# Local attention moved from GpSimd to TensorE and ScalarE, and q and k projected eight heads at a time

## The chip, the core and the metric

The kernel runs on one core of a Trainium2 chip. The core has five engines with a queue of instructions each, which run side by side and wait for one another by semaphores: TensorE (PE in the profile; PEld is its loading of weights), VectorE (DVE), ScalarE (ACT), GpSimd (POOL) and SyncE (SP), which here only issues DMAs. TensorE reads its operands from SBUF and writes into PSUM; a matmul can use a part of the array only, so that several small ones in different rows or columns run side by side. The metric is the device time of one execution in microseconds, as the median of several executions.

## The reference

```
x [1, 2048, 512];  32 heads of 16;  W, dil = 8, 2
g = sigmoid((x * gate_w).sum(-1))
a = A_ref(x, A_wqkv, A_wo)      # full attention, softmax over all 2048 keys
b = B_ref(x, B_wqkv, B_wo)      # local attention:
    idx = pos[:, None] - (arange(W) * dil)[None, :]     # 8 keys: s, s-2, ..., s-14
    logits = einsum("bhsd,bhswd->bhsw", q, k[idx]) * scale, -1e9 where idx < 0
    o = einsum("bhsw,bhswd->bhsd", softmax(logits), v[idx]);  b = o @ wo
out = g * a + (1 - g) * b
```

All arrays are bfloat16. A token of the local part sees only tokens of its own parity.

## The kernel before

**The global part** is cut into 32 periods: four chunks of 512 queries (`QW`) times eight groups of four heads (`NG`). A period has 16 tiles of 128 keys, so 64 units of one head's scores, 128 keys x 512 queries; the kernel has 2048 units. The scores are matmuls of 32 rows, one head in each quarter of the array. 16 of a head's 32 rows hold the head's dimensions; one further row carries a bound on the score in q and ones in k, so that no maximum over the keys is needed. A unit's exponential is taken by one of two engines. ScalarE does it exactly, three or two units at once out of two PSUM rings (`ring`, result `pT`). VectorE approximates it for four units at once, a quad (`make_quad`, lines 1310 to 1355): four conversions of scores into the bit pattern of a bfloat16 (`conv`, `dt<-m_ps`), then two added offsets (`term`, `dt<-dt`), the three versions being summed by the matmuls with V under weights (`WTS`, `vd_all`). At most `TD` = 4 of a period's 16 key tiles can go this way. The probabilities go into a matmul with V and a column of ones, 17 columns of the array for each head, into one PSUM bank (`acc`); `post` (line 912) turns the result, divides it by the sum (on GpSimd) and turns it back.

**Projections.** `k_proj` (line 520) and `q_proj` (line 619) do four heads at a time, each head's 16 columns in its own column quarter of the array. q also needs its magnitude (`absq`) and a second matmul with `selk` for the bound. `v_proj` (line 573) uses the full array.

**The local part** goes by 16 tiles of 128 tokens (`b_tile`, line 700). k, v and q are projected token-wise; k and v are stored to HBM (`kv_scr`) and loaded again eight times shifted (`ksh`, `vsh`, 1 MB each). GpSimd then multiplies, adds up trees, subtracts the maximum, normalises and weighs v, some 36 instructions a tile; VectorE gives the maximum, sum and reciprocal, ScalarE one small exp. The result (`obb`) is transposed by TensorE (`fin2`, `fin3`) and goes into `final` (line 962), which projects both parts with the output weights, mixes them by the gate and stores them.

**Order.** The class `Sched` (lines 118 to 328) is a planner that runs while the kernel is built. Every operation has an engine, an assumed duration, dependences, slots of buffers it takes and gives back, and a due time; the planner keeps a clock for each engine, always emits the operation that can start first, and among those that are near it the one due first. The order that comes out is the order of each engine's queue. `pe_source`, `act_source` and `d_source` offer the units of the attention: a fill of a ring for ScalarE (`fillA`) is due when ScalarE runs dry, and `start_quad` (line 1278) begins a quad when VectorE has less than 3 us of work waiting, fewer than three quads are under way and no TensorE operation is overdue. `warm` adds matmuls with zeros (`zero_pass`) where TensorE's recent streaming falls under a set share. `hooks(p)` (line 1388) runs when period p begins and sets up the projections and local tiles of later periods with due times in units of `TPER`, the planner's length of a period. Two PSUM banks (`m`) serve all other matmuls: projections, conversions and finals.

All instructions are recorded through one helper, so the profile shows line 382 (L382) for nearly all of them; groups are told apart by the names of their tiles.

Of the kernel before, what the change touches and what calls it, by code (L numbers as in the profile page):

```python
# [18 lines left out]
H = 32  # L19
# [5 lines left out]
NEG = -1.0e9  # L25
INF = 10 ** 12
# [7 lines left out]
TD = 4  # L34


def _mean_log_ratio():
    n = 4096
    acc = 0.0
    for k in range(n):  # L40
        y = 128.0 * k / n
        s = 0.0
        for o, w in zip(OFFS, WTS):
# [15 lines left out]
          ("ACT", "DVE"): 1000.0, ("DVE", "POOL"): 800.0, ("SP", "POOL"): 1500.0, ("POOL", "ACT"): 1000.0}  # L59
# [58 lines left out]
class Sched:  # L118
# [115 lines left out]
    def best(self, e):  # L234
# [14 lines left out]
        near = [c for c in cands if max(free, c[1]) <= soonest + 60.0]  # L249
# [82 lines left out]
def kernel(  # L332
# [13 lines left out]
    out2d = out.flatten_outer_dims()  # L346
    S, D = x2d.shape
# [56 lines left out]
    KEPT = 11  # L404
    for name_, n_ in (("m", 2), ("rA", 1), ("rB", 1), ("acc", 1), ("pTA", 3), ("pTB", 3), ("qt", 3), 
                      ("dt", 8), ("accT", 2), ("ott", 2), ("ksv", 2), ("prod", 1), ("lg", 2),
                      ("kvs", 1), ("qb", 1), ("osb", 3), ("keep", KEPT + 16), ("fb", 1)):
        S_.slots[name_] = Slots(n_)
# [15 lines left out]
    e32 = const.tile([128, 32], BF16, name="e32")  # L424
    V.memset(e32[:], 0.0)
    V.memset(e32[0:1, DH:DH + 1], 1.0)
    selq = const.tile([128, 128], BF16, name="selq")
    V.memset(selq[:], 0.0)
    for j in range(4):
        V.memset(selq[32 * j:32 * j + DH, 32 * j + DH:32 * j + DH + 1], 1.0)  # L430
    ident = const.tile([128, 128], BF16, name="ident")
    make_identity(nc, ident[:])

    wq = const.tile([128, DC, D], BF16, name="wq")
    wkv = const.tile([128, DC, 2 * D], BF16, name="wkv", tag="wkv")
    gw = const.tile([128, DC], BF16, name="gw")
    bw = const.tile([128, DC, 3 * D], BF16, name="bw")
    bwo = const.tile([128, DC, D], BF16, name="bwo")
# [4 lines left out]
    kmax_all = const.tile([128, NG, NC], FP32, name="kmax_all")  # L443
    kmax = const.tile([128, NG], FP32, name="kmax")
    selk_all = const.tile([128, NG, 128], BF16, name="selk_all")
    gate = const.tile([128, NT], FP32, name="gate")
    omg = const.tile([128, NT], FP32, name="omg")
    kv_scr = tc.dram_tile([16 + S, 2 * D], BF16, name="kv_scr")

    G.memset(vp_all[:, :, :, DH:DH + 1], 1.0)  # L450
    S_.t["POOL"] = 9000.0
# [6 lines left out]
    def x_load(half):  # L458

        def s():  # L460
            lo, hi = half * S // 2, (half + 1) * S // 2
            for c in range(DC):
                SP.dma_start(out=xT[:, c, lo:hi], in_=x2d[lo:hi, c * 128:(c + 1) * 128], transpose=True)
        return s
# [11 lines left out]
    for name, o, lo in (("wk0", wkv[:, :, 0:G1], D), ("wq0", wq[:, :, 0:G1], 0), ("wv0", wkv[:, :, D:D + G1], 2 * D)):  # L476
        with nc.allow_non_contiguous_dma(reason="columns of one head group"):
            A.dma_start(out=o, in_=a_w3[:, :, lo:lo + G1])
        ld[name] = S_.add(Op("SP", lambda: None, dur=1.0, due=-10.0, lat=4500.0, name=f"ld_{name}"))
    load("x0", x_load(0), 8100.0)  # L480
    load("x1", x_load(1), 11500.0)
    load("wv", dma(wkv[:, :, D + G1:2 * D], a_w3[:, :, 2 * D + G1:3 * D]), 9000.0)
    load("wk", dma(wkv[:, :, G1:D], a_w3[:, :, D + G1:2 * D]), 9000.0)
    load("wq", dma(wq[:, :, G1:D], a_w3[:, :, G1:D]), 9000.0)
# [5 lines left out]
    load("bw", dma(bw[:], B_wqkv.rearrange("(c p) n -> p c n", p=128)), 12000.0)  # L490

    def pad_load():
        for k in range(2 * D // 128):
            SP.dma_start(out=kv_scr[0:16, 128 * k:128 * k + 128], in_=zw[0:16, :])
    ld["pad"] = S_.add(Op("SP", pad_load, dur=4500.0, due=2000.0, lat=3000.0, name="ld_pad"))
    ld["bwo"] = S_.add(Op("SP", dma(bwo[:], B_wo.rearrange("(c p) n -> p c n", p=128)), dur=1500.0, due=2100.0, lat=6000.0, name="ld_bwo"))
    wo = []

    def wo_jobs(deps):

        def get():
            wo.append(const.tile([128, NG // 2, D], BF16, name="woarr", tag="wkv"))
# [15 lines left out]
    kt_ops = {}  # L518

    def k_proj(i, sc, due, first=False):  # L520
        hold = Hold("m")
        st = {}

        def part(c0, c1):
            def s():
                if c0 == 0:
                    st["pk"] = misc_ps(hold, [128, QW])
                    mm_init(st["pk"], e32, QW)
                pk = st["pk"]
                for c in range(c0, c1):  # L530
                    for j in range(4):
                        h = 4 * i + j
                        mm(pk[32 * j:32 * j + DH, :], wkv[:, c, h * DH:(h + 1) * DH],
                           xT[:, c, sc * QW:(sc + 1) * QW], False, c == DC - 1, tile_position=(0, 32 * j))
            return s

        def evac():
            o = kt_all[:, i, sc * QW:(sc + 1) * QW]
            if first:
                A.copy(out=o, in_=st["pk"][:])  # L540
            else:
                V.tensor_copy(out=o, in_=st["pk"][:])

        def red():
            src = st["pk"][:] if first else kt_all[:, i, sc * QW:(sc + 1) * QW]
            V.tensor_reduce(out=kmax_all[:, i, sc:sc + 1], in_=src, axis=AX.X, op=ALU.max, apply_absolute_value=True)
        slow = 2 if first and sc == 0 else 1
        p1 = Op("PE", part(0, 2), mms=COL4 * (3 * slow), deps=xt_ops[sc] + [ld["wk0" if i == 0 else "wk"]], due=due, acq=[hold], not_before=0.0 if first else due - 5000.0,
                name="k1")
# [928 lines left out]
```

## Time and profile before

| | us |
|---|---|
| median of three runs | 804.42 (801.79 to 805.17) |
| the profiled execution, its own time | 798.02 |
| its span, first to last instruction | 796.0 |
| TensorE's mean granted clock | 0.992 |
| GpSimd: sums and products for local attention (`prod`, three largest groups) | 268.9 + 161.7 + 152.2 |
| TensorE: local projections (768 matmuls), busy | 55.6 |
| TensorE: q projections (496 matmuls), busy | 36.0 |
| DMA traffic | 47.46 MB, mean 60 GB/s |

Busy time is the time in which at least one instruction of the group was running. Instructions of one engine overlap a little at their ends, and a matmul's 0.38 us are mostly its way through the array, while the next ones already stream; so a busy TensorE isn't a full one, and the distance from start to start says more.

### The profile page before, as it was taken

Reading aid. Unit: us, or ns where it says so; the run is one execution under the profiler, and the core shown is the slowest. Engines: PE = TensorE matmul, PEld = TensorE weight load, DVE = VectorE, ACT = ScalarE, POOL = GpSimd, SP = SyncE. Lnnn points to the kernel's source line nnn. Section 1 sums busy time; section 2 is a strip of 40 time slices with the busy share of each in tenths; the row PEclk is TensorE's granted clock in tenths of the full one; section 3 lists DMA queues with packets and bytes.
Section 4 is the critical chain, followed back from the end, with each engine's and each line's share of the span. In section 5 each row is a group of like instructions: output and inputs, shape, how many; then the busy total and the mean of one; then the engine's idle time right before and its main releaser. Section 6 shows DMA issues by size and latency. Waiting matters only on the chain.

```text
span 796.0 us, 20219 instructions
## 1 busy us (share of the span) xinstructions
PE 738.2 (93%) x8481; PEld 237.4 (30%) x8481; DVE 676.4 (85%) x1013; ACT 756.2 (95%) x680; POOL 695.4 (87%) x599
## 2 busy tenths in 40 slices
PE   7999999999999989999989899999999989999996
PEld 2332222333232223333322222333222222222222
DVE  3369899888989998989997888978998898888985
ACT  2899999899999999999999999999999999999993
POOL 1019799999999999999899999999998999999896
PEclk9799999999999999999999999999999999999999
DMA  9220321032011212111111121101122210122100
GB/s 206 88 68 12 109 67 55 18 104 68 22 47 54 68 54 68 55 50 42 45 68 54 54 67 54 65 18 55 56 67 81 68 54 30 53 68 67 61 15 34
DMA packets 52074, 47.46 MB, mean 60 GB/s; under 512 B 12048, under 2 KB 49424, under 8 KB 51984
## 3 DMA queue, kind: packets, MB, share of 16 engines
q1 hardware_dynamic: 50400, 45.98, 18.6%
q8 instruction: 66, 1.08, 0.6%
q10 hardware_dynamic: 1584, 0.20, 0.2%
q14 instruction: 24, 0.20, 0.1%
HBM read 37.75 MB, written 6.32 MB: 55 GB/s over the span
## 4 chain that ended last, share of the span: by engine, by line
ACT 29%; PE 28%; DVE 16%; POOL 16%; issue 9%; SPq 1%; DMA 0%; POOLq 0%; DVEq 0%; ACTq 0%
ACT pT L382 29%; POOL prod L382 13%; PE m_ps L382 13%; DVE dt L382 11%; PE acc L382 8%; PE ring L382 7%; SPq L382 1%; POOL lg L382 1%; DVE accT L382 1%; POOL obb L382 1%; POOL ott L382 0%; DVE kt_all L382 0%; DMA xT<-in_A_x_dram 0%; DVE kvs L382 0%; DVE vd_all L382 0%
## 5 line engine op out<-in xcount | busy, mean ns | idle before, releaser
L382 ACT ACTIVATE pT<-ring 128x1536 bf16<-128x1536 f32 (+1 forms) x658 | 750.1, 1316 | 13.2 <-PE ring L382 11.8
L382 PE MATMUL ring<-qt,kt_all 32*128 32x512 bf16 x1644 | 278.0, 383 | 31.0 <-ACT pT L382 25.3
L382 POOL TENSOR_TENSOR prod<-prod 128x512 f32<-128x512 f32 x224 | 295.2, 1324 | 10.8
L382 DVE TENSOR_SCALAR dt<-m_ps 128x512 uint16<-128x512 f32 x404 | 265.3, 676 | 26.8 <-PE m_ps L382 17.5
L382 DVE TENSOR_SCALAR dt<-dt 128x2048 uint16<-128x2048 uint16 x202 | 224.5, 1116 | 1.6 <-PE acc L382 1.0
L382 PEld LDWEIGHTS <-kt_all 32*128 32x128 bf16 (+1 forms) x2304 | 98.1, 91 | 293.1 <-issue 280.8
L382 POOL TENSOR_TENSOR prod<-ksh,qb 128x512 f32<-128x512 bf16 x128 | 161.7, 1292 | 5.6 <-DMA ksh<-kv_scr 3.3
L382 PE MATMUL acc<-pT,vp_all 128*17 128x512 bf16 x1644 | 158.1, 384 | 0.0
L382 POOL TENSOR_TENSOR prod<-vsh,lg 128x512 f32<-128x512 bf16 x128 | 152.2, 1208 | 3.5
L382 PE MATMUL m_ps<-qt,kt_all 32*128 32x512 bf16 x404 | 135.6, 381 | 5.8 <-DVE dt L382 4.5
L382 POOL TENSOR_TENSOR ott<-accT,rden 128x256 bf16<-128x256 f32 x31 | 25.0, 807 | 60.9 <-DVE rden L382 60.8
L382 PEld LDWEIGHTS <-vp_all 128*17 128x17 bf16 x2048 | 46.0, 88 | 107.4 <-issue 99.2
L382 PE MATMUL acc<-dt,vd_all 128*17 128x512 bf16 x808 | 61.1, 379 | 0.0
L382 PE MATMUL m_ps<-bw,xT 128*32 128x512 bf16 x768 | 55.6, 382 | 3.2 <-DVE dt L382 2.0
L382 PE MATMUL acc<-ones_t,zw 128*32 128x512 bf16 (+1 forms) x235 | 51.2, 391 | 1.3 <-DVE accT L382 1.2
L382 PEld LDWEIGHTS <-xT 128*32 128x32 bf16 (+1 forms) x1152 | 32.5, 97 | 32.9 <-issue 26.5
L382 PE MATMUL acc<-dt,vp_all 128*17 128x512 bf16 x404 | 39.6, 383 | 0.0
L382 PE MATMUL m_ps<-xT,wkv 128*16 128x512 bf16 x512 | 38.3, 388 | 1.2 <-DMA xT<-in_A_x_dram 1.2
L382 PE MATMUL m_ps<-xT,wq 128*16 128x512 bf16 x496 | 36.0, 380 | 0.0
L382 DVE TENSOR_SCALAR absq<-m_ps 128x512 int32<-128x512 int32 x31 | 21.3, 686 | 14.7 <-PE m_ps L382 14.4
L382 DVE CAST kt_all<-m_ps 128x512 bf16<-128x512 f32 x28 | 19.2, 687 | 13.3 <-PE m_ps L382 13.0
L382 PEld LDWEIGHTS <-zw 128*32 128x32 bf16 (+1 forms) x367 | 16.7, 94 | 42.7 <-issue 40.8
(72 smaller groups left out, 450.5 us busy)
## 6 DMA issues: line engine op xcount, KB each, us to landing
ksh<-kv_scr SPq DMA_DIRECT2D x16, 1024.0 KB, 5.5
vsh<-kv_scr SPq DMA_DIRECT2D x16, 1024.0 KB, 5.5
kv_scr<-kvs SPq DMA_DIRECT2D x16, 256.0 KB, 2.0
out_dram<-osb SPq DMA_DIRECT2D x16, 128.0 KB, 1.7
bw<-in_B_wqkv_dram SPq DMA_DIRECT2D x1, 1536.0 KB, 9.9
wkv<-in_A_wqkv_dram SPq DMA_DIRECT2D x2, 448.0 KB, 4.9
bwo<-in_B_wo_dram SPq DMA_DIRECT2D x1, 512.0 KB, 3.7
woarr<-in_A_wo_dram SPq DMA_DIRECT2D x8, 64.0 KB, 2.2
```

What stands on the lines that cost most here:

```text
L382: return chain_on(key, f(*a, **k))
```

## The change

Tokens are put in the order even, then odd, while x is loaded; the rest of the kernel works in that order, and the outputs are stored back by the same view. In this order a local query sees its own token and the seven before it. The 1024 queries of a parity are cut into two halves of nine blocks (57 queries, the last 56), and each block meets 64 keys (`KB`). For one head and one half a bank of PSUM holds 64 keys of the even tokens in partitions 0 to 63, of the odd ones in 64 to 127, by 512 queries: first a matmul of the identity with a band mask (`lmask`, -1e9 outside the band), then 18 matmuls of 32 rows and 64 columns (`l_fill`). That bank is one unit among ScalarE's (`act_units`, in a group of two, at least `LGAP` = 5 us apart); there are 64 of them. 18 matmuls of 64 rows and 64 columns weigh V and sum (`l_sum`), VectorE normalises. The result goes to HBM and comes back transposed by DMA (`l_back`).

q and k, of the global and the local part, are projected for eight heads at once with the full array (`pair_proj`); DMAs spread the heads over the 32-row quarters. k: VectorE copies and takes the maximum, then four DMAs per group of four heads. q: VectorE copies it and its magnitude, GpSimd multiplies the magnitude by the bound, two DMAs put both into HBM, and one DMA per group of four heads gets them back. The bound now takes 16 rows. The first group of four heads goes without DMAs (`k_first`, `q_first`, from weights doubled on VectorE). The V weights for VectorE's terms are made by GpSimd, for six key tiles instead of four. GpSimd keeps this, the multiplication of q, `ott`, and constants at the start.

```diff
-TD = 4
+TD = 6
...
-        near = [c for c in cands if max(free, c[1]) <= soonest + 60.0]
+        near = [c for c in cands if max(free, c[1]) <= soonest +
+                (300.0 if e == "PE" and c[0].mms[0][0] == self.pe_mode == "r" else 60.0)]
...
-                SP.dma_start(out=xT[:, c, lo:hi], in_=x2d[lo:hi, c * 128:(c + 1) * 128], transpose=True)
+                SP.dma_start(out=xT[:, c, lo:hi], in_=x3d[half, :, c * 128:(c + 1) * 128], transpose=True)
...
+    def pair_proj(w2, m, sc, due, hold, acq, deps, name):
...
+                    mm(st["p"][:], w2[:, c, 128 * m:128 * m + 128], xT[:, c, sc * QW:(sc + 1) * QW], c == 0, c == DC - 1)
...
+            def spread(sc=sc, st=st):
+                for e in groups:
                     for j in range(4):
+                        SP.dma_start(out=dst(e)[32 * j:32 * j + DH, sc * QW:(sc + 1) * QW], in_=st["r"][64 * e + DH * j:64 * e + DH * j + DH, :])
...
+            V.tensor_copy(out=st["r"][:, 0, :], in_=st["p"][:])
...
+            V.tensor_scalar(out=a_, in0=q_, scalar1=0x7FFF7FFF, scalar2=None, op0=ALU.bitwise_and)
...
+            G.tensor_scalar(out=st["r"][:, 1, :], in0=st["r"][:, 1, :], scalar1=kbnd[:, n:n + 1], scalar2=None, op0=ALU.mult)
...
+                SP.dma_start(out=_ap(r, [[32 * QW, 8], [QW, DH], [1, QW]]), in_=st["r"][:, two, :])
...
+                SP.dma_start(out=t_[:], in_=scr[e])
...
+                                mm(st[q_][64 * b:64 * b + 64, tt, :], xT[:, c, b * S // 2 + ks:b * S // 2 + ks + KB],
+                                   bv[:, c, 128 * m:128 * m + 128], c == 0, c == DC - 1, tile_position=(0, 64 * b))
...
+        mm(bank, ident[:], lmask[:, u, :], True, False, skip_group_check=True)
+        for k in range(NLT // 2):
+            a, w_, ks = l_block(u * NLT // 2 + k)
+            for b in range(2):
+                mm(bank[64 * b:64 * b + 64, 57 * k:57 * k + w_], kl_all[e][r:r + 32, b * S // 2 + ks:b * S // 2 + ks + KB],
+                   st["q"][2 * b + u][1][e][r:r + 32, 57 * k:57 * k + w_], False, True, tile_position=(r, 64 * b), skip_group_check=True)
...
+                    mm(st["p"][64 * b:64 * b + 64, k, :], pT[64 * b:64 * b + 64, s_, c0:c0 + 64],
+                       vl_all[hv.k][64 * b:64 * b + 64, u * NLT // 2 + k, h8, :], True, True, tile_position=(64 * b, 64 * b))
...
+            V.reciprocal(out=rl[:], in_=st["p"][:, :, DH:DH + 1].rearrange("p k o -> p (k o)"))
+            V.tensor_tensor(out=ob["t"][:, :, h8, :], in0=st["p"][:, :, 0:DH],
+                            in1=_ap(rl[:], [list(rl[:].ap[0]), [1, NLT // 2], [0, DH]]), op=ALU.mult)
...
+                SP.dma_start(out=obt_tiles[(c_, m)], in_=o_scr[c_ * QW:(c_ + 1) * QW, 128 * m:128 * m + 128], transpose=True)
...
-    TPER = 23500.0
+    TPER = 22000.0
+    LGAP = 5000.0
...
+            q_pair(periods[p + 2][0], periods[p + 2][1] // 2, now + 0.8 * TPER)
...
+        while b_next[0] < NPR and b_next[0] * 5.6 + 0.5 <= p:
+            l_pair(b_next[0], now + 1000.0)
```

`b_tile` with its GpSimd program, `q_proj`, `k_proj` and `selk` are deleted.

## The prediction

> **What bounds the kernel now.** I read the page's busy shares and slices first, then the groups by shape, then the waits, then the timeline of TensorE and VectorE.
>
> ```profile
> span 796.0 us, 20219 instructions
> PE 738.2 (93%) x8481; PEld 237.4 (30%) x8481; DVE 676.4 (85%) x1013; ACT 756.2 (95%) x680; POOL 695.4 (87%) x599
> ...
> ACT  2899999899999999999999999999999999999993
> ```
> ScalarE is full in nearly every slice. Its chain of exps sets the length; the chain of waits agrees (ACT 29%, PE 28%, DVE 16%, POOL 16%: four engines fed to the same end).
>
> ```profile
> L382 ACT ACTIVATE pT<-ring 128x1536 bf16<-128x1536 f32 x329 | 503.2, 1530 | 7.2 <-PE ring L382 6.4 <-PE acc L382 0.3
> L382 ACT ACTIVATE pT<-ring 128x1024 bf16<-128x1024 f32 x328 | 361.8, 1103 | 6.0 <-PE ring L382 5.5
> ...
> L382 DVE TENSOR_SCALAR dt<-m_ps 128x512 uint16<-128x512 f32 x404 | 265.3, 676 | 26.8 <-PE m_ps L382 17.5 <-PE ring L382 7.8
> L382 DVE TENSOR_SCALAR dt<-dt 128x2048 uint16<-128x2048 uint16 x202 | 224.5, 1116 | 1.6 <-PE acc L382 1.0
> ```
> A unit is one 128x512 block of scores. ScalarE takes 1644 of them, VectorE 404: 101 quads, each four conversions (`dt<-m_ps`) and two terms (`dt<-dt`). The planner starts a quad whenever VectorE has room, so what is freed on VectorE comes off ScalarE.
>
> ```profile
> 18.47 4.68 ACT L382 ACTIVATE pT<-ring 128x1536 bf16<-128x1536 f32 x4 [1.56 <-PE ring L382]
> ...
> 771.03 12.01 ACT L382 ACTIVATE pT<-ring 128x1024 bf16<-128x1024 f32 x11
> ```
> These rows of two timelines give ScalarE's first and last exps: 18.47 to 783.04, 764.6 us. Less some 5 us for the 16 small exps of local attention (16 x 0.473, partly overlapped), that is 0.462 us per unit; 12.9 us of tail follow.
>
> **ScalarE's side of the sum.** Local attention becomes 64 more units (4 pairs x 2 halves x 8 heads, the even tokens' keys in the upper 64 partitions and the odd ones' in the lower), and none of these can go to VectorE. With Q quads ScalarE has 2048 + 64 - 4Q units. The 16 small exps go (-5). The start loses the step |q| x bound: now the last keys' maximum ends at 16.29 and the first exp begins at 18.47 through two small VectorE operations, matmuls (0.41) and a 0.69 copy; after, through two small operations and a 0.25 one: -1.2. At the end GpSimd's `obb` (to 788.6), its transposes, copy and projection stand before the last outputs; without them the chain accT, ott, oat, last matmuls is left: -2.5. Span = 796 + 0.462 x (468 - 4Q) - 8.7 + s = 1003.5 - 1.848Q + s, with s for new stalls of ScalarE. At Q = 101 it would be 817: the change loses unless VectorE takes 12 quads more.
>
> **VectorE's side.** Out, by the rows' sums: `absq` and `qt` 43.7, `kt_all` copies and `kmax` 39.4, `selk` 3.9, `kvs` and `qb` 32.6, `mx`, `ssum`, `rr` 18.4, `obt` 6.6, weighted V (goes to GpSimd) 4.8: 149.4 us in 258 instructions. In: q of eight heads at once, 32 (16 global, 16 local) x (copy 0.68 + magnitude 0.3, between the 0.225 of a 128x272 and the 0.41 of a 128x512 copy) = 31.5; k likewise 32 x (0.687 + 0.678) = 43.7; local V 16 x 0.687 + 4 x 0.41 = 12.6; 64 normalisations 32; first group and bounds 6. A normalisation is not in the trace: reciprocal and multiply of 144 elements, at least two `rden` (0.235 each: 0.47), at most 0.235 plus the 1.14 of the last `ott` (256 elements, beside GpSimd); I take 0.5, because GpSimd will be idle, and keep 0.47 to 1.38, +56 us, for the range. Together 126 us in some 305. The rows sum to 726 against 676.4 busy: 0.05 of each instruction lies under its neighbour. So other work falls from 236 to 212, less 0.05 x 454: 189 us.
>
> A quad now costs 4 x 0.676 + 2 x 1.116. The terms:
>
> ```profile
> 55.52 0.69 DVE L382 TENSOR_SCALAR dt<-dt 128x2048 uint16<-128x2048 uint16 x1
> ...
> 56.73 1.67 DVE L382 TENSOR_SCALAR dt<-dt 128x2048 uint16<-128x2048 uint16 x1
> ```
> One operation takes 0.69 or 1.67. GpSimd's instructions begin at about that time (3.9 us busy from 40 to 60); I read the long ones as waiting for it. GpSimd keeps some 31 `ott` (0.62 to 0.81), 32 multiplies of q (1.2 to 1.3 by the 128x512 rows) and the V weights: some 75 us instead of 695, so I take 0.69, with 1.116 as the other bound. Quad: 2.70 + 1.38 - 0.30 = 3.78, before 4.85.
>
> VectorE was busy 639 of the 720 us from 60 to 780 (88.7%). Its waits for PE at `absq` 14.4, `kt_all` 15.5, `kvs` 7.3 become fewer, as projections halve; I take 90%. Then 189 + 3.78Q = 686 + 0.90 x (207.5 - 1.848Q): Q = 125.6, span 771 + s. The cap rises from 4 to 6 key tiles a period (128 to 192 quads), so it doesn't bind.
>
> **TensorE, which is the danger.**
>
> ```profile
> 144.77 0.39 PE L382 MATMUL ring<-qt,kt_all 32*128 32x512 bf16 x3
> 145.09 0.41 PE L382 MATMUL m_ps<-absq,selk_all 128*32 128x512 bf16 x4
> 145.33 0.39 PE L382 MATMUL acc<-dt,vp_all 128*17 128x512 bf16 x4
> ...
> 146.41 1.75 PE L382 MATMUL m_ps<-gw,xT 128*128 128x1 bf16 x64
> 148.09 0.41 PE L382 MATMUL m_ps<-ident,obb 128*32 128x128 bf16 x16
> 148.33 0.39 PE L382 MATMUL acc<-pT,vp_all 128*17 128x512 bf16 x4
> ```
> Start to start: four column tiles of 512 take 0.22 to 0.24, three row tiles 0.32, of which 0.105 is the change of tile shape; 64 tiny full-array matmuls take 26 ns each with a new weight each; 16 small column-tiled ones 15 ns each. Counted so over all matmul rows from 50 to 780: 457 us of streaming and 1259 changes (132 us), 589 of 730; some 42 us more where two row tiles collide (excesses of 0.2 to 0.3 us). 107 zero fillers are in it (some 43 us), which give way. So 588, 81%, is needed.
>
> Out: q with its zero and bound matmuls 41, k 30, local projections and transposes 45. In: q and k full-width 27, local q and k 28, local V 576 x 28 ns = 16, 25 quads 30, ScalarE's units -3, new shape changes 40 (three and a half per local unit, one per projection step). A local unit: mask 0.216 plus 18 score and 18 sum matmuls, each with its own weights, between 15 and 26 ns; I take 20, as they are tiled but only by two: 0.94, 60 us (48 to 74). Total 588 - 116 + 198 = 670, of some 705: 95% (93 to 97).
>
> The Trainium skill, "TensorE: Matmul & The Clock Gate", Part 3 on packing small matmuls, speaks against this: a weight load overlaps running matmuls only where the row group differs, and a unit's 18 score matmuls share one. By its P / 1.2 ns for a load of P = 64 columns, as an estimate 53 + 24 = 77 ns each, a local unit would be about 2.0 us and the span past 830. The 26 ns row, a full-array weight per matmul on all rows, disagrees, so I keep the trace's price.
>
> New stalls: ScalarE waited in 17 of 658 groups, 0.7 us each. A local fill is four times as long. None and all 64 are the bounds (0 to 45 us); one in ten gives s = 4.
>
> **Other queues.** SP gets some 400 issues of 0.33 to 0.5 us, 16 transposing loads (eight took 11.06) and 32 waits of about 2.0 us from put to get, in which the spreads behind them stand: near 230 us of 770. A q takes some 8.6 us (projection 0.9, copy and magnitude 1.0, GpSimd 1.3, two DMA hops of 2.7) and is due 0.8 period after a start, needed two periods after it: about 20 us of cover. Without it every pair would stop ScalarE by what is late.
>
> **Sum.** Span 771 + 4 = 775; the profiled execution lies 2.0 above its span: 777. The one of before, 798.02, lies 0.8% under the median of 804.42, so in medians 783.
>
> **Rivals.** (1) VectorE packs tighter: fewer slots held for long by q, no collisions with GpSimd. At 95%, and with 0.07 us of each instruction under its neighbour instead of 0.05, 180 + 3.66Q = 721 + 0.95 x (207.5 - 1.848Q): Q = 136, span 752, median 760. Against it: its `dt` waits for PE (26.8 us) have no reason to go. (2) TensorE becomes the bound, slower than before. Place: the local fills and sums beside the ring fills. Its share now is 81%, 87% with the fillers; I know no bound above that, and the forecast takes 95% as possible. Were 93% the most, quads would slip, and each lost quad gives the span 1.85, TensorE 1.7 more room and 0.5 less work. At 20 ns that costs about 11 (span 783); from there each 0.1 us per unit costs 6.4 us of TensorE and 5.3 of span; from about 29 ns per small matmul it is slower (span over 800). At 33 ns: 0.47 more, span 808, median 816. For it: the 26 ns floor. Against it: the 15 ns row. (3) The extra hops through SP arrive late: 16 pairs by 2 us, 32 us, median about 815; the 20 us of cover speak against it. (4) The gain is eaten: price 24 to 28 ns, median about 804.
>
> **Numbers.** Forecast 0.50, TensorE partly binding at a small gain (791 to 800) 0.08, (1) 0.15, (2) 0.16, (3) 0.04, (4) 0.07. No change is within 0.5%, 800.4 to 808.4, about what this kernel's runs can tell. Faster 0.73, same 0.07, slower 0.20. The forecast's own range is 768 to 797; with the tails of (1) and (2), 755 to 815.
>
> **What would show it.** Right: about 500 `dt<-m_ps` (125 quads), terms near 0.70, ScalarE still over 95%, `exp` groups about 1610 units. Wrong in the step on VectorE: Q under 115 with VectorE idle; on TensorE: local units over 1.4 us start to start and waits of ScalarE for `ring` far over 15 us; on SP: TensorE waiting for `qt`.

## The result, and the profile after

The changed kernel is slower: 868.4 us as the median of four runs (865.9 to 874.9) against 803.1 us (794.3 to 805.2) for the kernel before on the same chip, a ratio of 1.085 (95% interval 1.074 to 1.095). The forecast was 783 us. Executions that took over 1.5% longer than the fastest of the same kernel are called slow, and the times and comparisons below go by the others, while a profile, and the span and clock read from it, can be of a slow one. The profiled execution of the changed kernel took 870.4 us with a span of 868.6, which is 94 us over the forecast span of 775.

The page of the changed kernel, its busy times and three of its rows by slice (a slice is 21.7 us; the last row is the granted TensorE clock in tenths):

```profile
span 868.6 us, 22323 instructions
PE 786.0 (90%) x9360; PEld 275.9 (32%) x9447; DVE 646.3 (74%) x1153; ACT 763.6 (88%) x664; POOL 123.0 (14%) x118
...
ACT  2789996897798999976899999699779999999994
...
PEclk9789995896999999997899999899769999999998
```

Two things are new. ScalarE, full in nearly every slice before, has holes. And the clock row, which before showed 9 everywhere but in the second slice, falls in the same places (slices 7, 8, 10, 19, 20, 26, 29 and 30 are low in both). The mean granted clock went from 0.992 to 0.923. The clock row of before:

```profile
PEclk9799999999999999999999999999999999999999
```

The groups by shape (columns: count, busy us and mean ns of one, then the idle time ahead of them and what ended it):

```profile
L388 ACT ACTIVATE pT<-ring 128x1536 bf16<-128x1536 f32 x329 | 485.7, 1476 | 40.9 <-PE ring L388 37.6 <-PE m_ps L388 2.7
L388 ACT ACTIVATE pT<-ring 128x1024 bf16<-128x1024 f32 x328 | 343.7, 1048 | 37.8 <-PE ring L388 31.0 <-PE m_ps L388 5.1 <-ACT pT L388 0.3
L388 DVE TENSOR_SCALAR dt<-m_ps 128x512 uint16<-128x512 f32 x468 | 313.0, 683 | 87.4 <-PE m_ps L388 61.4 <-PE ring L388 23.7
...
L388 DVE TENSOR_SCALAR dt<-dt 128x2048 uint16<-128x2048 uint16 x234 | 158.5, 689 | 2.7 <-PE acc L388 0.8
...
L388 DVE TENSOR_TENSOR obb<-m_ps,rl 128x144 bf16<-128x144 f32 x64 | 19.7, 308 | 2.2
...
L388 PE MATMUL acc<-ones_t,zw 128*128 128x512 bf16 x43 | 17.9, 428 | 1.5 <-issue 1.5
...
L388 DVE RECIPROCAL rl<-m_ps 128x9 f32<-128x9 f32 x64 | 13.6, 213 | 12.2 <-PE m_ps L388 11.7
```

468 conversions are 117 quads, so ScalarE has 2048 + 64 - 4 x 117 = 1644 units, exactly as many as before: what VectorE took over is what local attention added. The exps themselves are no dearer; what grew is the idle time ahead of them, 78.7 us in place of 13.2, and 68.6 of it ended with TensorE filling a ring. The zero matmuls into `acc` fell from 107 to 43; their row before was

```profile
L382 PE MATMUL acc<-ones_t,zw 128*128 128x512 bf16 x107 | 38.2, 388 | 0.0
```

The waits of the changed kernel (us in total, times, longest), those of ScalarE and VectorE for TensorE and those that end with a DMA:

```profile
ACT pT L388 <- PE ring L388: 68.6, 88, 5.0
DVE dt L388 <- PE m_ps L388: 61.4, 83, 3.2
...
DVE qr L388 <- DMA lq_scr<-qr: 8.0, 4, 4.0
...
PE ring L388 <- DMA ql<-lq_scr: 6.6, 2, 4.5
...
DVE kr L388 <- DMA kl_all<-kr: 6.2, 2, 3.1
```

The first two before:

```profile
DVE dt L382 <- PE m_ps L382: 17.5, 38, 1.1
ACT pT L382 <- PE ring L382: 11.8, 17, 1.6
```

Before, waits of VectorE for a DMA there were none, and TensorE's matmuls waited for one only at the start, for x (1.2 us).

Two windows of 20 us show what the clock does (columns: us, then busy time of PE, PEld, DVE, ACT and POOL with counts, the granted clock, the DMA share, GB/s):

```profile
300.00:320.00 20.00, 18.74 (x263) 7.17 (x265) 16.77 (x32) 19.82 (x19) 0.62 (x1) 1.00 0.02 5
140.00:160.00 20.00, 20.00 (x184) 6.50 (x180) 8.91 (x17) 12.79 (x12) 0.00 (x0) 0.50 0.03 7
```

In the first, at full clock, ScalarE is busy 99% of the time. In the second, at half clock, TensorE is busy without a gap, gets 184 matmuls through in place of 263, and ScalarE starves at 64%.

**What sets the clock.** In the clock record of every run the granted clock is 1 or 0.5, and stretches of half clock between 40 and 780 us are multiples of 3.41 us (3.4, 6.8, 10.2, 13.7, 27.3). I cut each trace into windows of that length and took the share of the array's streaming in each: a matmul streams from its start for its columns at 2.4 per ns, at half clock at 1.2 per ns, and counts by the share of the array's rows and columns that it occupies, in steps of 32. So 1 is the most that the granted clock allows. Over all runs told of here, between 40 and 780 us, that is my count:

```
drops to half clock: 133; after a window with a share of 0.36 or less: 124 (the highest 0.38)
full-clock windows with no drop after them: 3280; of these with a share of 0.36 or less: 44
returns to full clock: 133; after a window with a share of 0.70 or more: 125
half-clock windows with no return after them: 339; of these with a share of 0.70 or more: 78
```

So it isn't standing still that goes ahead of a drop but streaming little: 29 of the 133 windows had TensorE busy for 90% or more. Coming back asks for about twice the share, but at half the clock: 0.70 of it is 0.35 of the full rate. In columns per window the two marks are nearly the same; at half clock TensorE has to stream for seven tenths of the window to reach it. The mark for coming back is the less sharp one. In the changed kernel 130 us between the first exp and the last lie at half clock (10 us before, all at the start). The windows ahead of these drops are of two kinds. In one, five of them with 41 us of half clock behind them, TensorE waits for a DMA or for VectorE that does; the timeline from 550 us (start, duration, engine, operation, and in brackets the idle time before and what ended it):

```profile
552.08 0.21 PE L388 MATMUL ring<-ql,kl_all 32*64 32x57 bf16 x1
554.79 0.80 SPq L388 DMA_DIRECT2D ql<-lq_scr  x2
...
556.83 0.37 PE L388 MATMUL ring<-ql,kl_all 32*64 32x57 bf16 x7 [4.55 <-DMA ql<-lq_scr]
```

A local fill has begun, its second q tile hasn't landed, and everything on TensorE stands behind it for 4.6 us. In the other kind, four with 75 us, TensorE is hardly idle, but the window holds a local unit, whose small matmuls take time and occupy little of the array. (The last 14 of the 130 us belong to the start.) The experiments weigh the two.

### The profile page after: what moved, and what is told of

The parts are those of the page before. It is cut to its first block, busy times and chain, and to the rows that moved or that the text cites. A ratio compares the mean times of both kernels' runs of the same rounds, so it can differ in the third digit from the quotient of the medians.

```text
span 868.6 us, 22323 instructions
## 1 busy us (share of the span) xinstructions
PE 786.0 (90%) x9360; PEld 275.9 (32%) x9447; DVE 646.3 (74%) x1153; ACT 763.6 (88%) x664; POOL 123.0 (14%) x118
## 4 chain that ended last, share of the span: by engine, by line
PE 44%; ACT 36%; issue 10%; DVE 4%; DMA 4%; SPq 1%; POOL 0%; DVEq 0%; ACTq 0%
ACT pT L388 36%; PE m_ps L388 17%; PE ring L388 14%; PE acc L388 13%; DMA lq_scr<-qr 2%; DVE dt L388 1%; SPq L388 1%; PE warm L388 1%; DMA qt<-q_scr 1%; DVE kt_all L388 1%; DVE qr L388 0%; DMA ql<-lq_scr 0%; DMA kl_all<-kr 0%; DVE kmax_all L388 0%; DVE qt L388 0%
## 5 line engine op out<-in xcount | busy, mean ns | idle before, releaser
L388 ACT ACTIVATE pT<-ring 128x1536 bf16<-128x1536 f32 (+1 forms) x658 | 759.8, 1261 | 78.7 <-PE ring L388 68.6
L388 DVE TENSOR_SCALAR dt<-m_ps 128x512 uint16<-128x512 f32 x468 | 313.0, 683 | 87.4 <-PE m_ps L388 61.4
L388 PE MATMUL m_ps<-qt,kt_all 32*128 32x512 bf16 x468 | 166.6, 403 | 11.0 <-DVE kr L388 5.1
L388 PE MATMUL acc<-pT,vp_all 128*17 128x512 bf16 x1580 | 158.5, 405 | 3.1 <-issue 3.0
L388 DVE TENSOR_SCALAR dt<-dt 128x2048 uint16<-128x2048 uint16 x234 | 158.5, 689 | 2.7 <-PE acc L388 0.8
L388 POOL TENSOR_SCALAR qr<-qr,kbnd 128x512 bf16<-128x512 bf16 x32 | 53.2, 1664 | 295.2 <-DVE qr L388 233.3
L388 PEld LDWEIGHTS <-xT 128*64 128x64 bf16 (+1 forms) x960 | 37.1, 109 | 15.7 <-issue 15.5
L388 PE MATMUL ring<-ql,kl_all 32*64 32x57 bf16 (+1 forms) x1152 | 31.9, 195 | 6.7 <-DMA ql<-lq_scr 6.6
L388 PE MATMUL m_ps<-vl_all,pT 64*64 64x17 bf16 x1152 | 30.5, 179 | 5.5 <-ACT pT L388 5.2
L388 PEld LDWEIGHTS <-kl_all 32*64 32x64 bf16 x1152 | 24.6, 111 | 30.5 <-issue 29.7
L388 PEld LDWEIGHTS <-pT 64*64 64x64 bf16 x1152 | 24.6, 113 | 25.1 <-ACT pT L388 13.7
L388 POOL TENSOR_SCALAR vd_all<-vp_all 128x272 bf16<-128x272 bf16 (+2 forms) x16 | 20.3, 1272 | 76.6 <-DVE vp_all L388 75.9
L388 PEld LDWEIGHTS <-vd_all 128*17 128x17 bf16 x936 | 23.7, 93 | 20.5 <-issue 3.1
```

The source lines that it names most:

```text
L388: return chain_on(key, f(*a, **k))
```

## The experiments

The clock theory (theory C in the expectations): the time is lost because TensorE's clock falls, through windows that stream too little. Its rivals: the work theory (theory P, or TensorE-is-full), the small matmuls, or TensorE's work altogether, cost more time than priced (the forecast's rival 2); the SP theory (theory S), SP's hops arrive late and cost what they are late (rival 3); the VectorE theory, VectorE never gets the quads.

"Median" is that of the executions compared. Span, first exp, "half" (the time at half clock between the first exp and the end of the last) and "idle" (ScalarE's idle time in that stretch) are of the profiled execution; the kernel before had 796.0, 18.5, 10, 12.0 and 101.

| run | median us | span | first exp | half | idle | quads |
|---|---|---|---|---|---|---|
| changed kernel | 868.4 | 868.6 | 20.3 | 130 | 77.0 | 117 |
| e1_sum_weight | 904.1 | 920.4 | 20.3 | 239 | 122.3 | 117 |
| e2_sp_times | 857.5 | 880.1 | 33.2 | 137 | 77.1 | 119 |
| e12_both | 849.8 | 848.4 | 20.3 | 96 | 62.4 | 120 |
| thr_more_zeros | 893.8 | 894.1 | 22.6 | 140 | 99.0 | 119 |
| e3_sum_waits_exp | 880.6 | 875.3 | 22.4 | 140 | 79.1 | 117 |
| f1_three_fixes | 846.3 | 841.5 | 28.3 | 51 | 49.2 | 120 |
| f1_zeros_in_unit | 871.4 | 870.9 | 20.3 | 79 | 86.8 | 121 |
| b_no_zeros (kernel before) | 829.5 | 845.0 | 18.6 | 167 | 53.0 | 103 |
| a_start_on_scalar | 852.9 | 845.0 | 19.6 | 58 | 57.3 | 117 |
| g0_start_and_fixes | 828.6 | 830.8 | 19.6 | 44 | 47.5 | 120 |
| g1_third_k_buffer | 836.1 | 838.7 | 21.7 | 68 | 51.0 | 120 |
| f1_no_small_matmuls | 799.2 | 810.2 | 29.4 | 17 | 22.9 | 120 |
| h0_no_dependence | 859.8 | 872.4 | 19.6 | 130 | 83.2 | 122 |
| h1_no_small | 816.3 | 811.8 | 21.7 | 14 | 29.4 | 122 |
| h2_scores_only | 832.8 | 839.0 | 19.6 | 68 | 54.1 | 122 |
| h3_four_quads | 852.2 | 864.5 | 21.7 | 113 | 72.7 | 119 |

**The planner's numbers.** The first three runs correct what the planner assumes. It adds zero matmuls where recent streaming falls under `STREAM` or `LEAST`, but it counts two small matmuls of a local sum as 60 columns on the whole array, seven times what they stream (2 x 17 columns on a quarter of it); and it takes SP's issues as shorter than they are in the trace of the changed kernel.

```diff
-                self.streamed.append((t, t + cols / 2.4, 1.0 if tile_ is None else 0.25))
+                self.streamed.append((t, t + cols / 2.4, 0.14 if m == "d" else 1.0 if tile_ is None else 0.25))
```

> The sums of the local part count in the planner's share of streaming as what they stream (0.14 of what they counted), so it adds zero passes around them: 141 instead of 106. Theory C (clock: windows of 3.4 us with too little streaming, made by local units, put TensorE to half clock): the half-clock stretches that began at a local unit (133, 198, 618, 669 us: 75 us) mostly go, those that began at a wait for a DMA (51, 236, 389, 406, 557 us: 41 us) stay; half clock after 50 us falls from 116 to 40 to 60 us, ScalarE's idle time after its first exp from 79 to about 55, time about 835 to 845. Theory P (TensorE simply has too much work, the clock only follows): zero passes make it worse, 870 or more. Theory S (SP's queue is the cause): within 1% of 868.

It went the other way: 904 us, 36 more, with 133 zero matmuls in place of 52 and 239 us at half clock. Five of the fourteen drops follow waits that lead back to a DMA (at 48, 393, 417, 574 and 584 us), seven others a window with a local unit or half of one, zeros or no zeros. Why it came out so much worse is open; that more zeros by the planner's count alone hold the clock is refuted, and the time lies where the work theory put it.

```diff
-            sps.append(S_.add(Op("SP", spread, dur=1150.0 * len(groups), lat=XQ,
+            sps.append(S_.add(Op("SP", spread, dur=2500.0 * len(groups), lat=XQ,
...
-                Op("SP", put, dur=1150.0, lat=XQ, allow=0.0, rel=[hr], name=name + "put"),
+                Op("SP", put, dur=1250.0, lat=XQ, allow=0.0, rel=[hr], name=name + "put"),
...
-            o_stored[key] = S_.add(Op("SP", store, dur=300.0, lat=3000.0, deps=list(ob["norms"]), rel=[ob["h"]], name="ost"))
+            o_stored[key] = S_.add(Op("SP", store, dur=3700.0, lat=3000.0, deps=list(ob["norms"]), rel=[ob["h"]], name="ost"))
...
-            obt_ops[(c_, m)] = S_.add(Op("SP", s, dur=100.0, lat=3500.0,
+            obt_ops[(c_, m)] = S_.add(Op("SP", s, dur=1320.0, lat=3500.0,
```

> The planner is given the issue times that SP showed (0.62 us per spreading DMA instead of 0.29, 3.7 us instead of 0.3 for a store of the local result, 1.32 instead of 0.1 for a transposing load). Theory S: waits for kr, qr, ql and qt on landing DMAs fall from some 27 us to under 8, the half-clock stretches that began at them (41 us) go, the others stay; time 835 to 845. Theory C alone, without SP: the same direction, since the stretches are started by these waits. Theory P: no change in the waits for ring, 860 to 870.

The DMA waits went: VectorE's 14.2 us of waiting for DMAs at `kr` and `qr` became 0.7, and no drop after the first 60 us has such a wait ahead of it. The time hardly told: 857.5 us, 11 less than the changed kernel. The first exp came 13 us later, so the hops may be worth up to 24 us. The profiled execution (881.9 us) shows none of that: its time at half clock stayed, 137 us, since seven windows with local work fell instead. The SP theory names something real, but 24 of the 85 us over the forecast are the most that this run gives it.

> Both edits. Theory C with S as its trigger: half clock after 50 us under 20 us, ScalarE idle under 30 us, 120 quads; time 800 to 815, so within 2% of before. Theory P: TensorE at full clock still keeps ScalarE waiting 60 us or more, 850 or above.

With both edits 849.8 us, ratio 1.060 (1.050 to 1.071): 19 us less, with 96 us at half clock where the clock theory, with SP as the trigger, asked for under 20.

```diff
-STREAM = 0.48
-LEAST = 0.42
+STREAM = 0.56
+LEAST = 0.5
```

> Only the planner's shares are raised (0.48 to 0.56, 0.42 to 0.50): 239 zero passes instead of 106, SP as it was. Theory C: stretches from local units go as in the first run and those from DMA waits stay: half clock after 50 us 40 to 60 us, time 840 to 855 because the passes take TensorE 28 us. Theory P: 880 or more. If the clock is full nearly throughout and the time still above 850, TensorE's work is the bound.

On the changed kernel this gave 230 zero matmuls and 893.8 us. The half-clock time did not shrink (140 us), and ScalarE's idle time outside these stretches and the windows ahead of them rose from 21 to 37 us. That is the work theory's forecast.

**The sums and their exp.** In the timeline TensorE often stands half a microsecond ahead of the local sums, because the planner lets them go before their exp has ended. The edit gives them the exp as a dependence:

```diff
-        o1 = S_.add(Op("PE", sums, mms=[("d", None, 60)] * (NLT // 2), allow=3000.0, deps=evs, acq=
+        o1 = S_.add(Op("PE", sums, mms=[("d", None, 60)] * (NLT // 2), allow=3000.0, deps=evs + [ex], not_before=ex.vis + 0.0, acq=
```

> Only the planning of the local sum changes: it may be planned no earlier than the end of its exp, on which it depends (so far the planner knew only its dependence on V). Theory: TensorE stands 0.5 us at the head of many of the 64 sums, in windows that hold a local unit as well, and that is what takes these windows under about 0.36 of streaming. Expected: waits of the sums for pT from 19 us to under 5, fewer half-clock stretches that begin at local units, those that begin at a DMA wait stay; half clock after 50 us 50 to 90 us (116), time 835 to 860. Rival (the small matmuls alone make the windows light): waits go, stretches stay, time within 1% of 868.

Alone it brought nothing (880.6 us), though the sums' waits for their exp, 18.9 us in the changed kernel, were gone. All three edits together, the weight corrected for the gate's matmuls too:

> SP's issue times, the sum's dependence on its exp, and the weights of sums and gate matmuls in the planner's share together. Clock theory: half clock after 50 us under 40 us and time 800 to 820; by the four runs so far time is about 791 + 0.57 per us of half clock, so 814 at 40 us. TensorE-is-full theory: over 845, as in the run with two of the fixes (848).

846.3 us, with half-clock time down to 51 us, though the first exp came 8 us late (28.3): four copies of weights on VectorE took 15.5 us there. The clock theory had asked for 800 to 820, the work theory for over 845, which the late start blurs.

**Work put into the local fill.** Two full zero matmuls in each local fill, on top of the three edits, raise the streaming of just those windows:

```diff
+        for _ in range(2):
+            mm(bank, zw[:], ones_t[:], True, True)
         mm(bank, ident[:], lmask[:, u, :], True, False, skip_group_check=True)
```

> As the run with three fixes, and each local fill streams two zero matmuls of 512 into its bank first: 64 x 0.43 = 28 us more work for TensorE, all in the windows that are light. Clock theory: half-clock stretches that begin at local units all but vanish (after 50 us under 20 us) and the time is not above that of the three fixes, 795 to 820. TensorE-is-full theory: 15 to 28 us slower than the three fixes.

871.4 us. All 57 local groups at full clock now wait for their fill, 39.6 us together, 0.69 each (14.0 us in 60 without the zeros). So what is added to a local fill is exposed to ScalarE nearly one to one, 25.6 of 28 us, as the work theory had it, and the clock can't be bought there: four of the six drops still follow a window with local work. In the changed kernel the fill as it stands was just covered: its 56 local groups at full clock waited 3.3 us together.

**The clock in the kernel before.** If the clock theory holds, taking the zero matmuls from the kernel before must cost time, although less work is left:

```diff
-    S_.filler = zero_pass
+    S_.filler = None
```

> The kernel before without its zero passes: 111 matmuls of 512 less, about 40 us of TensorE with their changes of shape. Clock theory: without them windows fall under 0.36 and the clock falls to half for tens of us: 815 to 850. Theory that TensorE's work counts: no slower than before, 785 to 803, since nothing but zeros was taken out.

It took 829.5 us, where the kernel before took 797.4 beside it. That is the clock theory's forecast, and the work theory's is refuted here. The clock row of its page, to be held against the row of nines shown before:

```profile
span 845.0 us, 20027 instructions
...
PEclk9986998997598899795979879999988969999899
```

With ScalarE given as much work as before (103 quads, 101 before), taking out 111 zero matmuls of some 0.39 us each cost 32 us; the profiled execution (847.0 us) had 167 us at half clock instead of 10.

**The start, and a third buffer.** The doubling of the first weights and the last step of the first keys go from VectorE to ScalarE:

```diff
-            V.tensor_copy(out=wd0[:, k, :, :, two, :], in_=w0[:, k].rearrange("p c (h d) -> p c h d", d=DH))
+            A.copy(out=wd0[:, k, :, :, two, :], in_=w0[:, k].rearrange("p c (h d) -> p c h d", d=DH))
...
-                A.copy(out=kt_all[:, 0, sc * QW:(sc + 1) * QW], in_=st[sc][:])
+                A.activation(out=kt_all[:, 0, sc * QW:(sc + 1) * QW], in_=st[sc][:], func=ACT.Identity, scale=isq[:], bias=isk[:])
```

> The changed kernel with two things of its start moved from VectorE to ScalarE: the doubling of the first weights, and the ones in the first group's k (now part of the copy out of PSUM). Theory: VectorE's copies wait for GpSimd's memsets (5.0 us for 4 copies here, 15.5 in the run with three fixes): first exp at 17.0 to 18.5 us instead of 20.3, the rest as it was, 862 to 870. Rival (the loads of x are late): first exp stays at 20 or later.

852.9 us on the changed kernel, though the first exp came only 0.7 us earlier, at 19.6 and not by 18.5: the order of all later work shifted, and 58 us at half clock were left instead of 130, with the DMA waits still there. Which windows fall hangs on small shifts; here that was worth 15 us, so single edits of this size prove little. With the three edits:

> The same on top of the three fixes: first exp at 17 to 18.5 us instead of 28.3, time 830 to 840 (846). Half clock as there (some 30 us after the start), unless it falls by chance elsewhere.

828.6 us, ratio 1.036 (1.018 to 1.054): the best version with all of the local work, and still slower than the kernel before.

```diff
-                      ("dt", 8), ("accT", 2), ("ott", 2), ("kl", 1), ("kr", 2), ("qr", 2), ("ql", 8), ("vl", 2), ("obb", 2),
+                      ("dt", 8), ("accT", 2), ("ott", 2), ("kl", 1), ("kr", 3), ("qr", 2), ("ql", 8), ("vl", 2), ("obb", 2),
```

> As before it, and three buffers instead of two for k on its way through SP, so that the first pair's spreads and the q of period 1 come earlier: the half-clock stretch at 46 to 58 us, present in nearly every run, goes, and with it 5 to 8 us: 820 to 832. If the remaining stretches vanish too, 800 to 810; if TensorE's work is the bound, no better than 835.

836.1 us, within g0's reach. The half-clock stretch at 48 us went, others came at 401, 439, 610 and 780 us.

**The small matmuls themselves.** The first attempt took them out of f1_three_fixes:

```diff
-        for k in range(NLT // 2):
+        for k in range(0):
...
-            for k in range(NLT // 2):
+            mm(st["p"][:].rearrange("p k d -> p (k d)"), pT[:, s_, 0:128], vl_all[hv.k][:, 0:NLT // 2, h8, :], True, True)
+            for k in range(0):
```

> The run with three fixes, leaving out the 18 score and 17 of the 18 sum matmuls of each local unit (mask, exp and normalisation stay; local attention is then not computed). The planned order is the same. TensorE has some 45 us less work but streams a little less too. TensorE-is-full theory: ScalarE's waits fall by over 20 us, time 800 to 815. Pure clock theory: windows are as light as before, the stretches stay, and the time is within 10 us of 846 less the start's excess of 8. In between: local units no longer keep ScalarE waiting at full clock (14 us there), stretches stay: 820 to 830.

799.2 us, 47 less than f1 and next to the work theory's 800 to 815; the profiled execution (812.1 us) had 17 us at half clock. The late start of both made this hard to size, so four more runs were made from one base: the start on ScalarE, SP's times and the weights, without the dependence (h0). h1 and h2 take the small matmuls out of h0, all of them or the sums alone, and keep the order of everything else.

> As g0_start_and_fixes (start on ScalarE, SP's times as measured, true weights of the sums and the gate's matmuls), but without the dependence of the local sums on their exp. Theory A (TensorE's work in a local fill is what ScalarE sees; the dependence put the sums of one group into the fill of the next): local groups wait under 10 us in all at full clock as in the changed kernel (3.3) and the time is 815 to 825. Theory B (the dependence is neutral, the half-clock stretches decide): within 8 us of 828.6, the difference going with the half-clock time at 0.57 us for each.

> The same order of instructions as h0_no_dependence, but the 18 score matmuls of a local fill and 17 of 18 sum matmuls are left out, so local attention is not computed. If the small matmuls cost time by themselves and through the clock, 25 to 32 us less than h0 and a half-clock time under 25 us; if f1_no_small_matmuls gained by its order alone, under 10 us less.

> The same order again; the 18 score matmuls stay and 17 of 18 sum matmuls are left out, so local attention is not computed. If the fill is the exposed part and the sums are covered, this is within 6 us of h0; if the sums, during which nothing else streams, are what drops the clock, it is nearer to h1 than to h0, with a half-clock time under 30 us.

h0: 859.8 us (857.1 to 862.5); h2: 832.8 (828.1 to 837.5); h1: 816.3 (813.4 to 819.7), ratio to before 1.019 (1.014 to 1.025). So the 64 x 18 sums cost 27 us and the 64 x 18 scores 16, together 43, more than the 25 to 32 expected. As the expectation for sums that drop the clock had it, h2 lies nearer to h1 than to h0, but its 68 us at half clock are not under 30. The rows of h0's page, then of h1's:

```profile
PE 801.0 (92%) x9440; PEld 279.5 (32%) x9528; DVE 657.0 (75%) x1175; ACT 758.0 (87%) x660; POOL 123.0 (14%) x118
...
PEclk9969985977999999999969969999999999979998
```

```profile
PE 726.1 (89%) x7212; PEld 240.6 (30%) x7288; DVE 653.6 (81%) x1175; ACT 749.1 (92%) x660; POOL 122.1 (15%) x118
...
PEclk9999999999999989999999999999999999999998
```

Without the small matmuls the clock row is whole again but for one slice and the last. How one local unit does it stands in h0's timeline of TensorE:

```profile
127.17 0.39 PE L388 MATMUL ring<-lmask,ident 128*128 128x512 bf16 x1
127.49 0.47 PE L388 MATMUL ring<-ql,kl_all 32*64 32x57 bf16 x18
127.89 0.39 PE L388 MATMUL ring<-qt,kt_all 32*128 32x512 bf16 x1
...
129.45 0.45 PE L388 MATMUL m_ps<-vl_all,pT 64*64 64x17 bf16 x18 [0.52 <-ACT pT L388]
129.84 0.39 PE L388 MATMUL m_ps<-xT,wk 128*128 128x512 bf16 x1
...
132.83 0.61 PE L388 MATMUL acc<-dt,vp_all 128*17 128x512 bf16 x4
```

From start to start the mask takes 0.32 us, the 18 scores 0.40, the 18 sums 0.39: 22 ns for each small matmul with the changes of shape. They were not dear each. All of them are still 64 x 0.79 = 51 us of TensorE's time, so h1 alone doesn't tell the work from the clock. But within 3.4 us they occupy 0.8, use at most an eighth of the array for the scores and a quarter for the sums, and 0.5 us of standing for the exp comes on top. That window has a share of 0.29; the clock falls right after it, and four `acc` matmuls that took 0.39 us take 0.61. Nine of the eleven drops of h0 between 60 and 780 us, but for 495.7 and 761.9, follow a window with a local unit or half of one.

The expectation on the dependence failed both ways. It is no cost, as that expectation's theory A had it: without it (h0) the kernel takes 31 us more than with it (g0), with 130 us at half clock instead of 44 in the profiled executions, and its local groups wait 13.2 us at full clock, not under 10. Yet alone, in e3, the same edit brought nothing. That it helps beside the other edits is measured, why not alone is open.

> h0_no_dependence with up to four quads under way in place of three. If the limit of three holds VectorE down, quads rise to 124 or more and the time falls by 1.85 us for each over h0's; if the two PSUM banks for conversions and projections do, quads stay at 117 to 122 and the time within 8 us of h0.

```diff
-        if e == "PE" and d_busy[0] < 3:
+        if e == "PE" and d_busy[0] < 4:
```

119 quads and 852.2 us, within the 8 us of h0: the limit of three is not what holds VectorE down. The two PSUM banks that conversions share with projections, sums and finals may be; VectorE's 61 us of waiting for `m_ps` fit, but a third wasn't tried.

**The sizes.** Over the eleven versions that do all the local work without extra zeros per fill or a raised threshold, with the first exp set to 20 us, a straight line fits: span = 811 + 0.45 x half-clock time, none off by more than 9 us. By it the changed kernel's 130 us at half clock are 58 us of its 94 over the forecast. The other 36, the 811 against 775, remain at full clock. The versions differ in more than the clock, though. Executions of one and the same program do not: the changed kernel's four spans go from 864.1 us at a mean granted clock of 0.932 to 873.1 at 0.917, by these clocks 118 and 145 us at half clock, so 0.33 us for each. All executions of all versions, each held against the mean of its own version, give 0.33 too. By that price the half clock is 43 of the 94 us. So the clock is, as an estimate, some 43 to 58 of them. The rest goes with TensorE's work, the start and the lost quads, and what each of these is worth stays open; thr_more_zeros and f1_zeros_in_unit, which gave TensorE more to do and came out slower, show that its work counts beside the clock.

h1 shows what this remainder is made of even with no small matmul. Its span is 15.8 us over that of before: the first exp 3.2 later (21.7 against 18.5), the tail after the last exp 4.4 longer (17.4 against 13.0), ScalarE's idle time 17.4 more (29.4 against 12.0), and 20 units fewer, -9.2 at 0.462 each. These add up to 15.8. Of the versions that compute everything, none reached the kernel before.

## Why the prediction was wrong

**The step that failed** is TensorE's: "107 zero fillers are in it (some 43 us), which give way", and with it the stall term, "one in ten gives s = 4". The fillers did give way, from 111 in all to 52. But they were not slack, they were what kept the clock (32 us without them in the kernel before): the work that replaced them takes TensorE's time and streams little. The forecast counted TensorE in microseconds, 95% of what there was, at full clock throughout. ScalarE's idle time was 77 us, 56 of them in stretches of half clock and the windows ahead of these, in place of the 16 that the sum contained (the 12.0 of before and s = 4).

**The price of the local unit was right.** 0.94 us plus changes of shape was forecast, 1.11 with them was measured. The Trainium skill's rule in "TensorE: Matmul & The Clock Gate", Part 3, and the price of a load that the prediction took beside it gave an estimate of 77 ns per score matmul; with 22 ns in h0's timeline the two can't both hold for these matmuls. The rule of the same page that did bear on this case, and that the prediction left aside, is in Part 1: the clock goes to half after an idle window of about 3.4 us. The run agrees in the length of the window, 3.41 us. It differs in what counts as idle: in the window at 127 us TensorE stood for 0.67 us only.

**VectorE.** The costs held: terms 0.689 (0.69 forecast), conversions 0.683, a normalisation 0.213 + 0.308 = 0.52 (0.50), and 175 us of other work (646.3 - 313.0 - 158.5; forecast 189). The share of 90% between 60 and 780 us didn't: 76% (544 of 720 us), and 83% in h1, where the clock is full but for 14 us. 117 quads in place of 125.6 are 8.6 x 1.85 = 16 us. The half clock can't be all of it: no version got past 122.

**ScalarE.** The form of the sum held, since Q = 117 gives 1644 units and exps that follow each other without a gap cost what they did (1.33 us from start to start for three units, 0.90 for two, in both kernels). Of the 94 us of span over the forecast 3 are the start, 1 the tail, 16 the 34 units that VectorE did not take and 61 the idle time over the 16. The remaining 13 come with the gaps: 138 of ScalarE's 664 instructions began after one, 40 of 680 before, and an exp after a gap no longer overlaps the one ahead of it. The start was missed: the first exp came at 20.3, not 17.3. The operation priced at 0.25 us took 1.82, and the four copies of weights ahead of it 5.04 us, while GpSimd was busy with its constants for nine tenths of that slice (the timeline of the start):

```profile
3.71 5.04 DVE L388 COPY obb<-obb 128x256 bf16<-128x256 bf16 x4
...
17.98 1.82 DVE L388 TENSOR_SCALAR qt<-qt,kbnd 128x512 bf16<-128x512 bf16 x1
```

The tail came at 11.4 us (10.4 forecast).

**SP.** "About 20 us of cover" failed in part: the direct waits for q and k are 21 us in all (8.0 + 6.6 + 6.2). The issues were longer than the 0.33 to 0.5 us assumed, 0.62 for a spread of k. At 373 us sixteen spreads hold the queue for 11.8 us (the timeline of SP), and at 384 us VectorE, and then TensorE, stand behind such a transfer:

```profile
373.56 11.82 SPq L388 DMA_DIRECT2D kl_all<-kr  x16
...
387.04 0.69 DVE L388 CAST kr<-m_ps 128x512 bf16<-128x512 f32 x1 [3.06 <-DMA kl_all<-kr]
...
387.78 0.37 PE L388 MATMUL m_ps<-qt,kt_all 32*128 32x512 bf16 x1 [2.22 <-DVE kr L388]
```

A drop of the clock followed five such waits, with 41 us at half clock, which the rival priced at nothing. But e2_sp_times removes nearly all of them and gains 11 us, at most 24, so rival 3 is a part of the cause at best.

**The rivals and the range.** Rival 2, TensorE as the bound at 808 to 816, had the place right, the local fills and sums, and TensorE's time does tell; but it knew one clock only and asked for a dear small matmul, and by its own sum 22 ns gives a span under 790. The range of 755 to 815 left out 868 because every case priced TensorE's work at one clock; and even without half clock the line leaves 811 us of span against 775. The row that spoke against that was in the page of before: 107 zero matmuls that compute nothing, in a kernel whose TensorE was 93% busy.

## What to carry to other kernels

Matmuls that compute nothing are not free room: ask what they hold up before giving their time to other work, and where the kernel plans such fillers, take them out of the kernel before to see the price. Count TensorE's work twice, once in time and once in the share of the array that streams within each few microseconds; work of small tiles adds to the first and takes from the second. When work moves to the engine that feeds the bound, its place in the order matters beside its sum: the local fills of the changed kernel were just covered, and zeros of an estimated 28 us put into such fills were seen by ScalarE nearly whole. To weigh a clock, compare executions of one program that were granted different clocks.

## What the runs showed of the hardware

- The granted clock is 1 or 0.5 and changes on a grid of 3.41 us. It drops after a window in which matmuls stream less than about 0.36 of the array, even with TensorE busy all the while, and returns after one with about 0.70 or more of what the half clock allows (124 of 133 drops, 125 of 133 returns; 44 windows under the first mark had no drop after them, 78 over the second no return).
- In columns the two marks are nearly one, 0.36 and 0.35 of the full rate, but at half clock TensorE needs twice the time for them: from 140 to 157 us of the changed kernel it was 100% busy with shares of 0.54 to 0.72, and the clock stayed at half.
- The granted clock differs between executions of one program, and the time with it: 0.951, 0.935, 0.924 and 0.923 in h0, with spans of 854.9, 860.4, 868.2 and 872.4 us.
- Small matmuls of one row group, each with its own weights, followed one another at 22 ns (18 in 0.40 us, with a change of shape).
- On the mean a 16-partition spread of k took SP 0.62 us to issue, each of the four DMAs that store a local half 0.93, a transposing load of their result 1.31.
